# Turning the queries of twenty token tiles by a DRAM round trip with one transposing transfer

## The chip, the cores and the metric

One core of one Trainium2 chip runs the whole kernel. The metric is device time in microseconds (us) of one execution; the profile's span runs from the first to the last instruction of the program on that core. TensorE (PE in the profile) does the matmuls, VectorE (DVE) and ScalarE (ACT) the work on elements, GpSimd (POOL) one small power per layer norm, and SyncE (SP) issues nearly all transfers.

## The reference

Two layers, each an FNet mixing step and then a PEER mixture of experts, on a sequence of 2048 tokens of width 512, in fp32:

```python
x = x + _A_ref(_layernorm(x), ...)      # y = Cr @ (x^ Wre^T) - Ci @ (x^ Wim^T), all dense
x = x + _B_ref(_layernorm(x), ...)
x = x + _A_ref(_layernorm(x), ...)
x = x + _B_ref(_layernorm(x), ...)

# _B_ref, per token (512 values), 32 heads, 16 + 16 keys, 256 experts:
q = einsum("nd,dhc->nhc", xf, w_q)                   # two halves of 128 for each head
s1, s2 = q1 @ k1.T, q2 @ k2.T                        # 16 scores for each half
i1, i2 = the two largest of s1, of s2                # 4 candidate sums and expert numbers
top_s, top_e = the two largest of the 4 candidates
g = softmax(top_s)
out = sum over heads and the two: g * gelu(xf . u[top_e]) * v[top_e]
```

## The kernel before

**Tiling.** The sequence is cut in 16 token tiles of 128 tokens. A layer is a list of nine units (`units`, in the order `ORDER[layer]`): seven of 256 tokens, which hold two token tiles each, and two of one token tile. `seq_unit` does the DFT along the sequence for one unit: for each of the 16 row blocks it loads a piece of the DFT matrix (`raw`), splits it on ACT and DVE in a high and a low part (`ch`, L458; `cl`, L462), and adds up three fp32r matmuls for each of four column blocks (L518). `token_tile` does all the rest for one token tile.

**One token tile.** In order: 24 matmuls for the DFT along the width (L668); the residual and a layer norm; the normed rows turned (for most tiles by a 32x32 block transpose on DVE, a store to `xdr` and four loads back, L722 to L745); scores against the folded keys (24 matmuls, L784 and L788); the experts' inner products with all 256 rows of u (L818) and their gelu; then on DVE a long chain that finds the two largest scores of each half (L880 to L926) and leaves in `q`, a [128 tokens, 3, 2, 2, 32] fp16 tile, for each of 128 picks (2 x 2 x 32) of each token the code of its first key, the code of its second key and its weight. These three 128x128 matrices are **the queries** of the change: picks lie along the free axis and have to come to the partitions. `f_pq` (L1015) turns them by three fp16 transposes on TensorE into a PSUM tile from the pool `bank`, and `f_qt` (L1020) copies that on ACT, rearranged, to the SBUF tile `qt`. From `qt` DVE makes four one-hot masks and two products (`f_m` and `f_w`, L1041 and L1047), TensorE multiplies them in 32 small matmuls (`f_blocks`, L1057), ACT takes the result out (L1089), and a second round trip through DRAM (`gdr`: two stores, L1116, and two loads, L1124) brings the expert weights into rows. These weight the gelu values (L1131); the product is turned (L1162) and multiplied with v (L1181, L1185), or, for most tiles of layer 1, put off to the end of the kernel.

**What sets the order.** Nothing is scheduled by the compiler. Each step is an `Op` of a `Plan` (`op(engine, us, fn, after, take, last, prio, lag, behind, shy)`): its engine, a written-in duration `us`, what it comes after, which buffers of a pool it takes and gives back, a priority, for transfers a `lag` until the data is there, and a further margin `shy` for those who use it. `Plan.run` plays this list forward in time, on each engine the step that can start first, by priority among equals, and never more than eight transfers in flight; the steps are then issued in the order of their planned starts. So each engine's order, SyncE's queue included, is fixed before the kernel runs; at run time an engine that comes to a step early waits there, and everything behind it in its queue waits too. A matmul step of a middle tile is planned another 0.8 us (`WARY`) after what another engine gives it. The matmuls of `seq_unit` have the lowest priority and fill TensorE between the steps of the token tiles.

The pools that the change touches or adds to: `bank` (4 PSUM banks), `q` (2 buffers), `qt` (1); beside them `raw` (4 loaded DFT pieces) and `c` (3 converted ones, of 12 matmuls each).

Of the kernel before, what the change touches and what calls it, by code (L numbers as in the profile page):

```python
# [11 lines left out]
F16 = mybir.dt.float16  # L12
# [4 lines left out]
P = 128  # L17
# [7 lines left out]
SP = 1  # L25
# [13 lines left out]

def MOVED(layer, at):  # L40
    return at >= 2 if layer == 0 else at < NCH + NSC * (TPC - 1) - 2


def DEFERRED(layer, at):
# [33 lines left out]
class Plan:  # L78
# [10 lines left out]
    def op(self, engine, us, fn, after=(), take=(), last=(), prio=(0, 0), lag=0.0, behind=(), shy=0.0):  # L89
        o = Op(len(self.ops), engine, us, fn, [a for a in after if a is not None], list(take), list(last), prio, lag,  # L90
               list(behind), shy)
        for h in o.last:
            h.users += 1
        self.ops.append(o)
        return o
# [60 lines left out]
MM512, MM256, TR32, TR16, MMG = 0.230, 0.121, 0.110, 0.057, 0.026  # L156
# [6 lines left out]
def act(n):  # L163
    return 0.09 + n / 1.2e3
# [7 lines left out]
def spectral_peer_kernel(ctx: ExitStack, tc, x_in, cseq, ctile, dhid, wq, k1t, k2t, ut, vm, out):  # L172
    nc = tc.nc
# [4 lines left out]
    dram = ctx.enter_context(tc.tile_pool(name="dram", bufs=1, space=bass.MemoryType.DRAM))  # L178
# [1 line left out]


    BUFS = {"acc": 4, "bank": 4, "raw": 4, "c": 3, "p": 1, "row": 4, "wr": 5, "wp": 2,
            "tok": 3, "sc": 1, "eq": 1, "act": 3, "q": 2, "top": 1, "qt": 1, "lr": 4, "gt": 1, "pp": 1, "gdr": 2, "xdr": 2, "bn": 1, "pick": 1}
    plan = Plan(BUFS)


# [41 lines left out]
    def work(shape, dtype, name, pool=None):  # L228
        return work_pool().tile(shape, dtype, name=name, bufs=BUFS[pool or name])
# [7 lines left out]
    op = plan.op  # L237
# [368 lines left out]
    last = {}  # L606
# [3 lines left out]
    def token_tile(layer, n, i, t0, at):  # L610

        prio = (0, layer, at if at < len(units) - 1 else -1 - layer, i)
# [5 lines left out]
        t = {}  # L618
# [6 lines left out]
        a = None  # L625
# [31 lines left out]
        for cs in wide:  # L657
            hb, nc_ = Hold("bank"), cs.stop - cs.start
            for z, (k, ms) in enumerate(steps):
                def f(z=z, k=k, ms=ms, cs=cs):  # L660
# [4 lines left out]
                    for c in range(2):  # L665
# [6 lines left out]
                a = op("PE", 2 * len(ms) * (MM512 if nc_ == D else MM256), f, [pready[layer, n][k][2 in ms], a] + dft_done + seed,  # L672
                       take=[hb] if z == 0 and not fine else [], behind=[a_row],
                       last=[phold[layer, n]] if z == len(steps) - 1 else [], prio=prio)
# [11 lines left out]
        if fine:  # L686
            a = ln_rest(lambda: t["bn"].rearrange("p a b -> p (a b)"), hbn, i, bn_done, prio)
        else:
            a = ln_stats(lambda: t["row"], i, [b] + ([xready[1, i]] if (1, i) in xready else []), prio)
# [60 lines left out]
        for z, k in enumerate([] if moved else ks):  # L750
# [16 lines left out]
            hb = Hold("bank")  # L767
            a = op("PE", (k.stop - k.start) * TR32, f_tr, [xn[z]], take=[hb], last=[hx], prio=prio)
# [7 lines left out]
        for hf in range(2):  # L776
            hb = Hold("bank")
# [21 lines left out]
            if fine:  # L799
                for z, k in enumerate(ks):  # L800
                    a_pe = op("PE", 2 * (k.stop - k.start) * MM512, lambda f=f_pch, hf=hf, k=k: f(hf, k), [a_th[z], a_pe],
                              take=[] if z else [hb], prio=prio)
# [8 lines left out]
        hb, hact, hg = Hold("bank"), Hold("act"), Hold("act")  # L811
# [13 lines left out]
        a = op("PE", 12 * MM256, f_xu, [a_pe], take=[hb], last=[hth, htl], prio=prio)  # L825
        a = op("ACT", act(N), f_act, [a], take=[hact], last=[hb], prio=late)
# [6 lines left out]
        a = op("ACT", act(N), f_g0, [a], take=[hg], prio=late)  # L833
        a = op("ACT", act(N), lambda: nc.scalar.activation(t["g0"], t["g0"], AF.Copy, bias=1.0), [a], prio=late)
        a = op("DVE", dve(N), lambda: nc.vector.tensor_mul(t["g0"], t["g0"], t["act"]), [a], prio=late)
        a = op("ACT", act(N), lambda: nc.scalar.activation(t["g0"], t["g0"], AF.Tanh, scale=C0), [a], prio=late)
        a = op("ACT", act(N), lambda: nc.scalar.activation(t["g0"], t["g0"], AF.Copy, bias=1.0), [a], prio=late)
# [3 lines left out]
        heq, hq, htop = Hold("eq"), Hold("q"), Hold("top")  # L841
# [91 lines left out]
        if fine:  # L933
            left, a_val, a_key, first = [], [], [], []
            for f in range(2):
                part = slice(f, f + 1), slice(f * H, (f + 1) * H), 32
                order_ = prio + (f,)
                a = largest(0, *part[1:], lambda f=f: t["pc", f], scored[f:f + 1], order_, **hold, behind=first)
# [5 lines left out]
                a = eq(0, *part[1:], view, a, order_)  # L944
                a = code(0, *part, a, order_)
                left += without(*part, view, a, order_, last=banks[f:f + 1], take=[] if f else [hsc])
                hold = {}
                a = tree32(1, *part[1:], left[f:], order_)
                a_val += a
                a = eq(1, *part[1:], lambda c=part[1]: flat("sc")[:, :, c], a, order_, last=[hsc])  # L950
                a_key += code(1, *part, a, order_)
        else:
            a = tree32(0, cols, w, sc_parts, prio, **hold)
            a = eq(0, cols, w, lambda: flat("sc"), a, prio)
            a = code(0, fs, cols, w, a, prio)
            a = without(fs, cols, w, lambda: flat("sc"), a, prio)
            a_val = tree32(1, cols, w, a, prio)
            a = eq(1, cols, w, lambda: flat("sc"), a_val, prio, last=[hsc])
# [48 lines left out]
        c5 = op("DVE", 0.13, lambda: nc.vector.tensor_sub(t["q"][:, 2, :, 1], t["gw"], t["q"][:, 2, :, 0]), [c4], last=[htop], prio=prio)  # L1007
        d0 = op("DVE", 0.1, f_df, a_key, prio=prio)
        d1 = op("DVE", 0.1, lambda: nc.vector.tensor_mul(t["df"], t["df"], t["cc"]), [d0, b6], prio=prio)
        d2 = op("DVE", 0.15, f_sel, [d1], last=[htop], prio=prio)  # L1010


        hb, hqt = Hold("bank"), Hold("raw" if fine else "qt")
# [8 lines left out]
            nc.scalar.copy(t["qt"].rearrange("p r (q j) -> p r q j", q=16),  # L1022
                           t["pq"].rearrange("p r (j q) -> p r q j", q=16))

        a = op("PE", 3 * TR16 + 0.06, f_pq, [c5, d2], take=[hb], last=[hq], prio=prio)
        a_qt = op("ACT", act(384), f_qt, [a], take=[hqt], last=[hb], prio=prio)

        def row_of(r, hf):
            m = t["qt"][:, r].rearrange("p (a b) -> p a b", b=4)[:, 16 * hf:16 * hf + 16]
# [6 lines left out]
        for hf in range(2):  # L1036
            for r in range(2):
# [6 lines left out]
                a = op("DVE", dve(1024, 2), f_m, [a_qt], take=[] if fine and r else hls[-1:], prio=soon)  # L1044
# [48 lines left out]
        if fine:  # L1093
            pe = [op("PE", 16 * MMG + 0.15, lambda hf=hf: f_blocks((hf,)), [made[hf]], take=hbs[hf:hf + 1],
                     last=hls[2 * hf:2 * hf + 1], prio=prio) for hf in range(2)]
# [3 lines left out]
        for hf in range(2):  # L1099
            if fine:  # L1100
                own = [op("DVE", 0.7, f_mask, xn[-1:], prio=late)] if hf == 0 else []
                evac.append(op(("ACT", "DVE")[hf], (1.26, 0.75)[hf], f_own(hf), pe[hf:hf + 1] + own, behind=evac, take=[] if hf else hgs[:1],
                               last=hbs[hf:hf + 1], prio=prio))
# [5 lines left out]
        moves, back = [], []  # L1109
        for hf in range(0 if fine else 2):  # L1110
            def f_out(hf=hf):
                if hf == 0:
                    t["gdr"] = dram.tile([2, E, 4, ROW], F32, name="gdr", bufs=BUFS["gdr"])
                d = t["gdr"][0]
                d = bass.AP(d.tensor, d.offset + hf * 8 * STEP, [[ROW, P], [STEP, 8], [1, 4 * E]])
                nc.sync.dma_start(d, t["gs", hf].rearrange("p g t e -> p g (t e)"))  # L1116
            moves.append(op("SP", 0.6, f_out, evac[hf:hf + 1], behind=moves[-1:], take=[] if hf else [hd], last=[hgs[hf]], prio=prio, lag=2.7))
        for j in range(0 if fine else 2):
            def f_in(j=j):
                if j == 0:  # L1120
                    t["gt"] = work([P, E, E], F32, "gt")
                d = t["gdr"][j]
                d = bass.AP(d.tensor, d.offset, [[STEP, 64], [4 * ROW, E], [1, E]])
                nc.sync.dma_start(t["gt"][j * 64:(j + 1) * 64], d)  # L1124
            back.append(op("SP", 0.6, f_in, moves, behind=back, take=[] if j else [hgt], last=[hd], prio=prio, lag=3.2, shy=0.5))
        if fine:
            a = op("PE", PICKS, f_picks, evac, take=[hgp], last=hgs[:1], prio=prio)
            a = op("DVE", dve(N), lambda: nc.vector.tensor_mul(t["act"].rearrange("p (e f) -> p e f", f=E), t["act"].rearrange("p (e f) -> p e f", f=E),
                                                               t["gp"].rearrange("p f e -> p e f")), [a, a_act], last=[hgp], prio=prio)
        else:  # L1130
            a = op("DVE", dve(N), lambda: nc.vector.tensor_mul(t["act"], t["act"], t["gt"].rearrange("p e f -> p (e f)")),  # L1131
                   back + [a_act], last=[] if deferred else [hgt], prio=prio)

        hb, hpp = Hold("bank"), Hold("c" if fine else "pp")
# [40 lines left out]
        hb = Hold("bank")  # L1175
# [169 lines left out]
```

## Time and profile before

| | us |
|---|---|
| median of 3 runs (lowest to highest) | 1233.59 (1233.14 to 1234.08) |
| the profiled execution | 1233.48 |
| its span | 1231.7 |
| TensorE busy in it | 1220.1 |
| VectorE busy | 1000.1 |
| ScalarE busy | 492.2 |
| transposes of the queries on TensorE (96, of which 60 belong to the twenty tiles) | 11.0 |

The durations of matmuls in the profile overlap, because they are pipelined: a matmul of 512 columns is listed with 0.39 us, but the next one starts 0.23 us later. What a matmul costs TensorE is read from the starts of its neighbours. The profiled execution's time and the median of the runs differ by 0.11 us; the span leaves out 1.8 us of the profiled execution's time.

### The profile page before, as it was taken

The numbers are of one execution on the slowest core, as the hardware profiler recorded it, in microseconds if no ns is written. First come the engines' busy times: TensorE is split into PE (matmuls) and PEld (weight loads), VectorE is DVE, ScalarE is ACT, GpSimd is POOL, SyncE is SP. The second block draws the span as 40 slices with busy tenths as digits, with TensorE's granted clock in tenths as the row PEclk, the third lists the DMA queues.
The fourth block names the chain that finished last, engine by engine and source line by source line (L and its number), as shares of the span: only waits on it lengthen the run. The fifth ranks groups of instructions, "written<-read, shape, count | busy, mean of one in ns | idle before, by whom it ended". The sixth has DMA issues, their size and how long they took to land. (4 is left out here: it accounts for less than half of the span.)

```text
span 1231.7 us, 20733 instructions
## 1 busy us (share of the span) xinstructions
PE 1220.1 (99%) x7626; PEld 1014.5 (82%) x7626; DVE 1000.1 (81%) x2272; ACT 492.2 (40%) x1010; POOL 45.0 (4%) x71
## 2 busy tenths in 40 slices
PE   9999999999999999999999999999999999999998
PEld 6877778878788888899988988788888888888886
DVE  8899997999897785968987359959596786859796
ACT  7522234334343333324654233334343333343455
POOL 2000000000000000000000000000000000000000
PEclk9999999999999999999999999999999999999999
DMA  7866551453444244441656243563635254454464
GB/s 241 261 200 218 188 169 35 101 119 83 123 122 113 70 116 116 107 120 49 172 142 174 79 120 82 125 135 92 154 97 140 73 145 111 99 141 104 115 204 144
DMA packets 312726, 160.12 MB, mean 130 GB/s; under 512 B 216752, under 2 KB 283056, under 8 KB 312624
## 3 DMA queue, kind: packets, MB, share of 16 engines
q1 hardware_dynamic: 312480, 158.66, 48.2%
q8 instruction: 60, 0.98, 0.3%
q14 instruction: 42, 0.34, 0.1%
q10 hardware_dynamic: 144, 0.13, 0.0%
HBM read 120.73 MB, written 38.01 MB: 129 GB/s over the span
## 5 line engine op out<-in xcount | busy, mean ns | idle before, releaser
L518 PE MATMUL acc<-ch,xh 128*128 128x512 f32 (+1 forms) x868 | 328.3, 378 | 0.8 <-DVE ptl L547 0.8
L518 PE MATMUL acc<-cl,xh 128*128 128x512 f32 (+1 forms) x868 | 321.9, 371 | 0.0
L518 PE MATMUL acc<-ch,xl 128*128 128x512 f32 (+1 forms) x868 | 321.7, 371 | 0.0
L458 ACT CAST ch<-raw 128x512 fp32r<-128x512 f32 x256 | 158.6, 620 | 272.0 <-PE acc L518 222.7
L462 DVE TENSOR_TENSOR cl<-raw,ch 128x512 fp32r<-128x512 f32 x256 | 176.0, 688 | 61.6 <-ACT ch L458 51.4
L518 PEld LDWEIGHTS acc<-cl,xh 128*128 128x128 f32 x868 | 163.6, 188 | 28.8
L518 PEld LDWEIGHTS acc<-ch,xh 128*128 128x128 f32 x868 | 163.6, 189 | 28.0 <-issue 1.8
L518 PEld LDWEIGHTS acc<-ch,xl 128*128 128x128 f32 x868 | 163.8, 189 | 25.6
L880 DVE TENSOR_TENSOR tmp<-sc 128x512 f32<-128x512 f32 (+1 forms) x64 | 43.5, 680 | 72.9 <-ACT sc L793 72.6
L784 PE MATMUL bank<-wh,tok 128*128 128x512 f32 x256 | 100.3, 392 | 0.3 <-ACT tok L742 0.3
L784 PE MATMUL bank<-wl,tok 128*128 128x512 f32 x256 | 99.7, 389 | 0.0
L668 PE MATMUL bank<-dh,pth 128*128 128x512 f32 x248 | 98.6, 397 | 0.0
L668 PE MATMUL bank<-dl,pth 128*128 128x512 f32 x248 | 96.7, 390 | 0.0
L668 PE MATMUL bank<-dh,ptl 128*128 128x512 f32 x248 | 93.6, 390 | 0.0
L793 ACT COPY sc<-bank 128x512 f32<-128x512 f32 x62 | 36.1, 588 | 138.1 <-PE bank L788 108.0
L1041 DVE TENSOR_TENSOR lr<-iota,qt 128x1024 f16<-128x1024 f16 x124 | 81.0, 686 | 12.0 <-ACT qt L1022 11.9
L260 POOL TENSOR_TENSOR stats<-stats,half 128x1 f32<-128x1 f32 x64 | 43.7, 689 | 1149.1 <-DVE stats L257 1135.1
L867 DVE TENSOR_TENSOR eq<-sc,val 128x1024 f16<-128x1024 f32 (+1 forms) x64 | 77.2, 1207 | 1.5
L518 PE MATMUL acc<-ch,xg 128*128 128x512 f32 (+1 forms) x204 | 77.3, 379 | 0.0
L518 PE MATMUL acc<-cl,xg 128*128 128x512 f32 (+1 forms) x204 | 75.7, 371 | 0.0
L518 PE MATMUL acc<-ch,xm 128*128 128x512 f32 (+1 forms) x204 | 75.7, 371 | 0.0
L788 PE MATMUL bank<-wh,tok 128*128 128x512 f32 x256 | 68.4, 389 | 0.0
(190 smaller groups left out, 2057.8 us busy)
## 6 DMA issues: line engine op xcount, KB each, us to landing
raw<-in_cseq SPq DMA_DIRECT2D x224, 256.0 KB, 2.8
wr<-in_wq SPq DMA_DIRECT2D x32, 512.0 KB, 3.8
gdr<-lr SPq DMA_DIRECT2D x62, 256.0 KB, 3.7
raw<-in_ctile SPq DMA_DIRECT2D x32, 256.0 KB, 2.9
xdr<-lr SPq DMA_DIRECT2D x25, 256.0 KB, 2.8
tok<-xdr SPq DMA_DIRECT2D x100, 64.0 KB, 2.6
wr<-in_x SPq DMA_DIRECT2D x16, 256.0 KB, 3.3
row<-in_x SPq DMA_DIRECT2D x16, 256.0 KB, 4.0
```

Of the source, the lines that this page charges most:

```text
L260: nc.gpsimd.tensor_tensor(st[:, 1:2], st[:, 1:2], half, op=ALU.pow)
L458: nc.scalar.copy(t[1], t[0])
L462: nc.vector.tensor_sub(t[2], t[0], as32(t[1]))
L518: nc.tensor.matmul(target(d), w[s][:, d * P:(d + 1) * P], moving(s % per, part), start=(s == 0 and k == 0 and d % blocks == 0), stop=(s == ...
L668: nc.tensor.matmul(t["y", cs.start], w[:, k, c, t0:t0 + P], r[:, c, k, cs], start=(not fine and z == 0 and c == 0 and m == 0), stop=(z == ...
L784: nc.tensor.matmul(t["pc", hf], t["th"][:, k, :], r[:, k, hf], start=(k == 0 and r is wh), stop=False)
L788: nc.tensor.matmul(t["pc", hf], t["tl"][:, k, :], wh[:, k, hf], start=False, stop=(k == KD - 1))
L793: nc.scalar.copy(t["sc"][:, :, hf, :], t["pc", hf].rearrange("p h e -> p e h"))
L867: nc.vector.tensor_tensor(t["eq"][:, :, cols], scores(), val(rank_, cols), op=ALU.is_equal)
L880: nc.vector.tensor_max(t["tmp"][:, :, cols], flat("sc")[:, :8, cols], flat("sc")[:, 8:, cols])
L1041: nc.vector.tensor_tensor(t["m", hf, r], io2, row_of(r, hf), op=ALU.is_equal)
```

## The change

For the units at places 2 to 6 of either layer's order (`Q_MOVED`), all of two tiles, so for 2 x 5 x 2 = 20 of the 32 token tiles, `f_pq` is not called. Instead SyncE issues a store of `q` to a DRAM tile `qdr` (3 matrices of 128 tokens by 128 picks; runs of 256 bytes, 96 KB), waits for it, and issues one transfer with `transpose=True` that reads the 384 x 128 fp16 elements back as 128 x 384 into a new SBUF tile `qi`. `f_qt` then copies from `qi`, and no longer from PSUM; what follows is as before. The plan is told 0.45 us and a lag of 2.3 us for the store, and 0.5 us, a lag of 3.0 us and a margin of 0.5 us for the load. The other twelve tiles keep the transposes on TensorE.

```diff
+def Q_MOVED(layer, at):
+    return 2 <= at < 7
...
-            "tok": 3, "sc": 1, ... "gdr": 2, "xdr": 2, "bn": 1, "pick": 1}
+            "tok": 3, "sc": 1, ... "gdr": 2, "xdr": 2, "qi": 1, "qdr": 2, "bn": 1, "pick": 1}
...
-        a = op("PE", 3 * TR16 + 0.06, f_pq, [c5, d2], take=[hb], last=[hq], prio=prio)
-        a_qt = op("ACT", act(384), f_qt, [a], take=[hqt], last=[hb], prio=prio)
+        if Q_MOVED(layer, at):
+            hqi, hqd = Hold("qi"), Hold("qdr")
+
+            def f_out():
+                t["qdr"] = dram.tile([3, P, P], F16, name="qdr", bufs=BUFS["qdr"])
+                nc.sync.dma_start(t["qdr"].rearrange("r t c -> t r c"), t["q"].rearrange("p r k a h -> p r (k a h)"))
+
+            def f_in():
+                t["pq"] = work([P, 3, P], F16, "qi")
+                nc.sync.dma_start(t["pq"].rearrange("p r t -> p (r t)"), t["qdr"].rearrange("r t c -> (r t) c"), transpose=True)
+
+            a = op("SP", 0.45, f_out, [c5, d2], take=[hqd], last=[hq], prio=prio, lag=2.3)
+            back = [op("SP", 0.5, f_in, [a], take=[hqi], last=[hqd], prio=prio, lag=3.0, shy=0.5)]
+            a_qt = op("ACT", act(384) + 0.05, f_qt, back, take=[hqt], last=[hqi], prio=prio)
+        else:
+            a = op("PE", 3 * TR16 + 0.06, f_pq, [c5, d2], take=[hb], last=[hq], prio=prio)
+            a_qt = op("ACT", act(384), f_qt, [a], take=[hqt], last=[hb], prio=prio)
```

More of the change, by code (lines that the diff above doesn't have):

```diff
@@ L182, in spectral_peer_kernel @@
     BUFS = {"acc": 4, "bank": 4, "raw": 4, "c": 3, "p": 1, "row": 4, "wr": 5, "wp": 2,
-            "tok": 3, "sc": 1, "eq": 1, "act": 3, "q": 2, "top": 1, "qt": 1, "lr": 4, "gt": 1, "pp": 1, "gdr": 2, "xdr": 2, "bn": 1, "pick": 1}
+            "tok": 3, "sc": 1, "eq": 1, "act": 3, "q": 2, "top": 1, "qt": 1, "lr": 4, "gt": 1, "pp": 1, "gdr": 2, "xdr": 2, "qi": 1, "qdr": 2, "bn": 1, "pick": 1}
     plan = Plan(BUFS)
```

## The prediction

> **What bounds the kernel now.** I read the page's first part, then stretches of the span, then who waits on TensorE.
>
> ```profile
> span 1231.7 us, 20733 instructions
> PE 1220.1 (99%) x7626; PEld 1014.5 (82%) x7626; DVE 1000.1 (81%) x2272; ACT 492.2 (40%) x1010; POOL 45.0 (4%) x71
> core 0: us, PE busy (x) PEld busy (x) DVE busy (x) ACT busy (x) POOL busy (x), PEclk, DMA share, GB/s
> 0.00:290.00 290.00, 285.15 (x2058) 228.48 (x2059) 269.93 (x538) 117.64 (x230) 20.61 (x32) 1.00 0.56 167
> 290.00:610.00 320.00, 318.79 (x1943) 270.22 (x1942) 259.01 (x622) 121.41 (x253) 13.16 (x19) 1.00 0.42 108
> 830.00:1150.00 320.00, 320.00 (x1745) 264.01 (x1744) 248.09 (x578) 118.04 (x248) 4.85 (x9) 1.00 0.46 114
> ```
>
> The twenty tiles' transposes lie in the stretches 290 to 610 us (layer 0) and 830 to 1150 us (layer 1). There TensorE is busy 318.79 of 320 and 320.00 of 320 us, at a full clock, while DVE has 61 and 72 us to spare and ACT some 200 in each. So TensorE's own work is the time: what leaves its queue shortens the span, as long as nothing new makes it wait.
>
> **What the transposes cost TensorE.** The group of L1018 shows 223 ns for one, but that is a pipelined length. The cost is read from the starts around a group of three, in the timeline (start, us, engine, line), at one tile among 512-column matmuls and at one behind 256-column matmuls:
>
> ```profile
> L1018 PE MATMUL bank<-ident,q 128*128 128x128 f16 x96 | 11.0, 223 | 0.4 <-DVE q L985 0.3
> 353.17 0.39 PE L518 MATMUL acc<-ch,xh 128*128 128x512 f32 x1
> 353.40 0.39 PE L518 MATMUL acc<-ch,xl 128*128 128x512 f32 x1
> 353.62 0.39 PE L518 MATMUL acc<-cl,xh 128*128 128x512 f32 x1
> 353.85 0.34 PE L1018 MATMUL bank<-ident,q 128*128 128x128 f16 x3
> 354.00 0.48 PE L518 MATMUL acc<-ch,xh 128*128 128x512 f32 x1
> 354.32 0.39 PE L518 MATMUL acc<-ch,xl 128*128 128x512 f32 x1
> ...
> 428.04 0.28 PE L818 MATMUL bank<-ul,tok 128*128 128x256 f32 x1
> 428.16 0.28 PE L818 MATMUL bank<-uh,tok 128*128 128x256 f32 x1
> 428.28 0.34 PE L1018 MATMUL bank<-ident,q 128*128 128x128 f16 x3
> 428.43 0.47 PE L518 MATMUL acc<-ch,xh 128*128 128x512 f32 x1
> 428.74 0.39 PE L518 MATMUL acc<-ch,xl 128*128 128x512 f32 x1
> ```
>
> At the first, two steps without transposes take 0.45 us (353.17 to 353.62) and the two steps that hold the three transposes take 0.70 (353.62 to 354.32): 0.25 us more. At the second, 428.16 to 428.74 is 0.58 us; without the transposes it would hold one step of 0.12 (428.04 to 428.16) and one of 0.225, so 0.235 us more. I take 0.24 us for a tile, 80 ns a transpose. Twenty tiles: **-4.8 us** on the engine that sets the time. The ends by the two readings are -4.7 and -5.0.
>
> **What it adds.** Two SyncE issues, a wait of SyncE between them, and a chain from `q` to `qt` that is longer by a round trip. The nearest rows are the two round trips that the kernel has: each tile's `gdr`, and `xdr` in 25 tiles (KB each, median us to landing; then one line's issue time in ns and its landing as min/median/max):
>
> ```profile
> gdr<-lr SPq DMA_DIRECT2D x62, 256.0 KB, 3.7
> tok<-xdr SPq DMA_DIRECT2D x100, 64.0 KB, 2.6
> x2d<-row SPq DMA_DIRECT2D x16, 256.0 KB, 2.0
> gt<-gdr SPq DMA_DIRECT2D x62, 64.0 KB, 3.0
> ptd<-pp SPq DMA_DIRECT2D x52, 64.0 KB, 2.2
> wr<-in_dhid SPq DMA_DIRECT2D x4, 512.0 KB, 4.5
> L1116 SPq DMA_DIRECT2D gdr<-lr x62: 366/418/1491, 221.5 to 1207.4; - x62
> DMA to landing us min/median/max: 2.6/3.7/5.1
> L735 SPq DMA_DIRECT2D tok<-xdr x100: 562/628/845, 268.3 to 1101.6; - x100
> ```
>
> *The store* (96 KB, runs of 256 B) lies between `x2d<-row` at 2.0 and `gdr<-lr` at 3.7, which has the same runs and 2.7 times the bytes; `ptd<-pp`, 64 KB in shorter runs, is nearest, at 2.2. I take 2.5 us. *The transposing load* has no row at all. As a plain load of its size it would take 2.6 to 3.0 (`tok<-xdr`, `gt<-gdr`); the slowest median of the table is 4.5, and no row bounds it above. I take 3.3, little over the plain loads of its size, and keep 2.6 and 4.5 as ends for the forecast. Round trip: 5.8 us (4.6 to 8.2).
>
> The plan in the code allows 0.45 + 2.3 for the store, 0.5 + 3.0 + 0.5 for the load and two hops of 0.1: 6.95 us. At 5.8 the data comes 1.15 us early. Between data and TensorE there is more cover, as the small matmuls L1057 of `f_blocks`, the first on TensorE to need `qt`, stand behind DVE's last product L1047 with a margin (the plan's 0.8 us of `WARY` and a hop):
>
> ```profile
> 433.53 0.69 DVE L1047 TENSOR_TENSOR lr<-lr,qt 128x1024 f16<-128x1024 f16 x1
> 435.45 0.69 PE L1057 MATMUL bank<-lr 128*64 128x64 f16 x32
> ...
> 456.54 0.67 DVE L1047 TENSOR_TENSOR lr<-lr,qt 128x1024 f16<-128x1024 f16 x1
> 458.64 0.69 PE L1057 MATMUL bank<-lr 128*64 128x64 f16 x32
> ```
>
> The margins are 435.45 - 434.22 = 1.23 and 458.64 - 457.21 = 1.43 us; I use 1.3. So a round trip of up to 6.95 + 1.3 = 8.25 us costs TensorE nothing, and beyond that each us late is one us of TensorE for each tile. The upper end, 8.2, is just inside.
>
> *Who waits behind the new wait.* SyncE stands about 2.5 us at the load until the store is in; loads of DFT pieces are queued behind it. ACT comes to the copy to `qt` and waits if the data is late, with casts `ch` (L458) behind it; DVE then waits at L1041, with `cl` (L462) behind it. All three lead to the matmuls L518. The cover is the queue of pieces:
>
> ```profile
> L458 ACT CAST ch<-raw 128x512 fp32r<-128x512 f32 x256 | 158.6, 620 | 272.0 <-PE acc L518 222.7 <-issue 21.3 <-PE bank L518 14.2
> ...
> ACT ch L458 <- DMA raw<-in_cseq: 5.7, 4, 2.7
> SPq L1124 <- DMA gdr<-lr: 44.5, 29, 3.8
> ```
>
> ACT waits 222.7 us for TensorE to give a converted piece back, so in general two are ready ahead, 2 x 12 x 0.227 = 5.4 us of matmuls. SyncE stands 29 times, up to 3.8 us, at the same kind of wait for `gdr`, and ACT has waited for a piece's data only 5.7 us in the whole span. I cost these waits at nothing; without the cover it would be 2.5 us a tile, 50 us in all.
>
> *What round trips cost TensorE in practice.* Its waits at the first matmuls behind such trips, and two rows for the small items below:
>
> ```profile
> L1162 PE MATMUL bank<-identf,act 128*128 128x128 f32 x38 | 7.5, 278 | 1.2 <-DVE act L1131 1.2
> L784 PE MATMUL bank<-wh,tok 128*128 128x512 f32 x256 | 100.3, 392 | 0.3 <-ACT tok L742 0.3
> L544 ACT CAST pth<-acc 128x512 fp32r<-128x512 f32 x62 | 36.4, 587 | 36.4 <-PE acc L518 36.3
> q1 hardware_dynamic: 312480, 158.66, 48.2%
> ```
>
> TensorE waited 1.2 us at L1162 behind `gdr`, over 18 tiles (38 transposes, two a tile, less the last tile, which has no such trip), and 0.3 us at L784 behind `xdr`, over its 25 tiles (100 loads, four a tile): 1.5 / 43 = 0.035 us a trip, so **+0.7 us** for twenty.
>
> *Small items together, at nothing.* SyncE issues 40 more transfers at 0.42 and 0.63 us, 21 us of a queue that mostly waits. The copy to `qt` reads SBUF instead of PSUM, about 33 ns dearer by 620 against 587 (0.7 us over twenty tiles, on an engine busy 40%). The 3.9 MB are 2.5% on 158.66 MB, at 48.2% of the transfer engines. `q` is held some 2.5 us longer, with two buffers. A bank of PSUM comes free earlier, but no wait above is for one; it could gain at most the 1.2 us that TensorE idles in the layer 0 stretch. The whole order is planned anew, so steps move that the change doesn't name; I have no row for that but those idle times, and it goes into the chances.
>
> **Sum.** Span 1231.7 - 4.8 + 0.7 = 1227.6; the 1.8 us around it (1233.48 for the profiled execution) give 1229.4; the median of the runs lies 0.11 above that execution: **1229.5 us**. Its own range is 1227.5 (no added wait, and the 1.2 us of idle gone too) to 1231.1, which is 0.2% below before. That 2.5 us is about what a measurement of this kernel can tell from no change.
>
> **Rivals.** *A, the transposing load is slow (slower).* If the load carries its three 128-column blocks one after another, each at the price of a small transfer of its own, it takes 3 x 2.2 = 6.6 us (the `ptd` row). The trip is then 2.5 + 6.6 = 9.1, and TensorE waits 9.1 - 8.25 = 0.85 us at L1057 of every tile, 17 us: 1229.5 + 17 = 1246.5. It decides from a load of about 5.95 us, where 20 x 0.2 us eat the gain; slower by 0.2% from 6.1 (20 x 0.33). For it: no row shows a transposing load. Against it: it would have to land later than any median here, later than even the slowest `gdr` store (5.1).
> The Trainium skill speaks for A. "VectorE: DVE Perf Modes", section "The three transpose paths", gives 1309 ns for a 128x128 bf16 transpose by DMA and 390 ns on TensorE, and its rules advise TensorE where PSUM will do. Three such blocks on top of a plain load of 2.6 us would be an estimated 6.5 us, and the time about 1244.5. The trace does not bear out its TensorE figure for this use: 80 ns each in a running queue. "Advanced Engine Details and Errata", section "X-Bar Transpose (TRN2)", says the contrary for DMA, that such transfers are as fast as regular ones; by that the time is 1229.5. No run here shows either.
>
> *B, the gain is eaten (no change).* The chain grows by 5.8 us, so `f_m` and `f_w` of a unit's second tile, six DVE steps of 0.69 us, move into the next unit's layer norms and block transposes, and these come later. If TensorE waits 0.1 to 0.35 us a tile for that, 2 to 7 us come back: 1231.1 to 1236.1, middle 1233. For it: in 0 to 290 us, where DVE is 93% busy, TensorE idles 4.85 us. Against it: the 61 and 72 us that DVE has spare.
>
> *C, SyncE's queue is held (slower).* If the transposing issue and its wait hold SyncE for more than the 5.4 us of pieces ahead, matmuls L518 starve. At 6.4 us it is 1 us a tile, 20 us: 1249.5. Against it: issues of 0.42 and 0.63 us, and four more pieces in `raw`.
>
> **Chances.** Forecast 0.58: TensorE is full where the change acts, and the round trips here cost almost nothing. B 0.18. A 0.18, for want of any row of such a load. C 0.06. So faster 0.58, no change 0.18, slower 0.24. Of A, half lies over 1246; with C 0.15 is left out above, and 0.04 below 1227.5. Range 1227.5 to 1246.
>
> **What the profile after would show.** L1018 with 36 instead of 96 transposes, the busy time of TensorE in the two stretches still over 99.5%, `qi<-qdr` landing within 4.5 us, ACT's waits for it under some 10 us in all, and no wait of PE at the small matmuls: right. PE waits at L1057's successor released by DVE, together over 4 us: A. Waits of ACT casts for `raw`: C. New PE idle at the score matmuls or the transposes of `act`: B. The most likely way to be wrong is the load's unseen price.

## The result, and the profile after

| | before | changed |
|---|---|---|
| median of 20 runs, us | 1233.93 | 1236.43 |
| lowest to highest | 1233.14 to 1235.36 | 1233.73 to 1237.29 |
| span of the profiled execution | 1231.7 | 1234.8 |

The ratio is 1.0019, with a 95% interval of 1.0013 to 1.0025: the change made the kernel 2.5 us slower, on the very edge of what was called telling from no change. 1229.5 was forecast. Among the runs below, one of the sixteen-tile kernel (3106.65 us) and one of the kernel before (1498.69 us) were slow; the ratios leave them out, and the sixteen-tile median of 1232.39 us would be 1232.24 without that run. All line numbers from L41 on are higher in the changed kernel: by 4 up to the queries, by 19 behind them (the matmuls L518 are L522, the small matmuls L1057 are L1076).

The page's first part and the two stretches in which the transposes lay, of the changed kernel:

```profile
span 1234.8 us, 20688 instructions
PE 1217.6 (99%) x7566; PEld 1012.7 (82%) x7566; DVE 1001.3 (81%) x2272; ACT 498.1 (40%) x1010; POOL 48.7 (4%) x71
...
290.00:610.00 320.00, 318.24 (x1894) 270.83 (x1894) 254.31 (x612) 122.67 (x249) 11.97 (x18) 1.00 0.46 113
830.00:1150.00 320.00, 318.79 (x1712) 263.51 (x1711) 248.72 (x580) 122.73 (x252) 5.39 (x9) 1.00 0.49 121
```

TensorE has 60 instructions fewer and is busy 2.5 us less, but the span is 3.1 us longer. These two stretches lost little: 1.76 us of idle instead of 1.21, and 1.21 instead of none. The rest of the loss lies in a stretch that the prediction didn't quote, the end of layer 0. Before:

```profile
600.00:700.00 100.00, 99.66 (x636) 86.02 (x635) 72.55 (x163) 49.77 (x93) 3.56 (x5) 1.00 0.53 143
```

and after, with who released TensorE there in the view of waits (us in all, times, longest):

```profile
600.00:700.00 100.00, 96.30 (x605) 81.49 (x604) 74.10 (x170) 48.59 (x92) 6.95 (x5) 1.00 0.57 145
...
PE acc L522 <- DVE xl L291: 2.1, 2, 1.7
PE bank L1076 <- DVE lr L1066: 0.8, 1, 0.8
PE bank L788 <- ACT tok L746: 0.4, 1, 0.4
PE bank L1022 <- DVE q L1011: 0.3, 1, 0.3
```

TensorE idles 3.70 of these 100 us, before 0.34. The longest waits are for `xl`, the low part of a normed tile with which layer 1 begins: layer 0's last tiles come in late.

Such idle time understates the loss, for a matmul is listed for 0.39 us and the next could start after 0.23, so each wait hides 0.16 us. I therefore also went from start to start: the time from each matmul to the next, less the median step of its kind in the kernel before. By this measure the changed kernel loses 4.8 us more than before between 600 and 700 us, 1.0 more from 300 to 600, 1.5 more from 750 to 1150, and 0.6 in the rest; with the 4.8 us of the transposes gone (the slower matmul behind each group counted with them), the span grows by 3.1, which is what the page shows. The experiments below use both measures; "lost" is the one from start to start, in one profiled execution each.

Most of the transfers went well. Issues (KB, median us to landing), the issue time of the transposing one in ns with its landing, and the copies to `qt`:

```profile
qdr<-q SPq DMA_DIRECT2D x20, 96.0 KB, 1.8
qi<-qdr SPq DMA_TRANSPOSE x20, 2.4
...
L1038 SPq DMA_TRANSPOSE qi<-qdr x20: 1133/1150/1280, 304.3 to 1144.1; - x20
...
L1026 ACT COPY qt<-qi 128x384 f16<-128x384 f16 x20 | 19.0, 950 | 1.8 <-DMA qi<-qdr 1.8
L1026 ACT COPY qt<-bank 128x384 f16<-128x384 f16 x11 | 5.3, 479 | 5.5 <-PE bank L1022 5.5
L1076 PE MATMUL bank<-lr 128*64 128x64 f16 x992 | 22.3, 197 | 2.8 <-DVE lr L1066 2.1 <-ACT lr L1108 0.7
```

The store takes 1.8 us and the transposing load 2.4, by the medians. But the load issues for 1.15 us, the copy from `qi` takes 0.95 us where the copy from PSUM takes 0.48, and TensorE now waits 2.1 us at the small matmuls for DVE's products. One trip, in the timeline of DVE, ACT and SyncE:

```profile
577.17 0.22 DVE L1011 TENSOR_TENSOR q<-gw,q 128x64 f16<-128x64 f32 x1
577.42 0.39 SPq L1034 DMA_DIRECT2D qdr<-q  x1
579.25 1.15 SPq L1038 DMA_TRANSPOSE qi<-qdr  x1
...
582.92 0.62 ACT L462 CAST ch<-raw 128x512 fp32r<-128x512 f32 x1 [2.25 <-PE acc L522]
583.45 0.95 ACT L1026 COPY qt<-qi 128x384 f16<-128x384 f16 x1
```

The load is issued 1.8 us after the store and its data is there at about 581.6 (579.25 + 2.3), but the order lets ACT do the copy only behind a cast that itself waits 2.25 us for TensorE. Of the 7.0 us from `q` to `qt`, 1.9 are the place in ACT's queue and 0.95 the copy.

One store was slow: that of the second tile to take the trip, issued at 326.79 us, landed after 5.3 us, and the load's data was there at 334.42. That is 8.9 us after `q` was ready (325.55). There ACT waits for the load, DVE for ACT's copy and TensorE for DVE:

```profile
325.32 0.23 DVE L989 TENSOR_TENSOR q<-key,df 128x128 f16<-128x128 f16 x1
...
qdr<-q SPq DMA_DIRECT2D x1, 96.0 KB, 5.3
...
334.44 0.93 ACT L1026 COPY qt<-qi 128x384 f16<-128x384 f16 x1 [1.26 <-DMA qi<-qdr]
335.40 1.89 DVE L1060 TENSOR_TENSOR lr<-iota,qt 128x1024 f16<-128x1024 f16 x3 [3.10 <-ACT qt L1026]
339.76 0.44 PE L1076 MATMUL bank<-lr 128*64 128x64 f16 x16 [0.61 <-DVE lr L1066]
```

These 1.26 us are most of the 1.8 us that ACT waits for loads in all, and the 0.61 us are one of the three waits that make the 2.1 us; the others are 0.80 at 655 us and 0.71 at 1094 us. Why this store is slow is not shown; in the kernels below that move the same tile in the same way it takes about as long (5.0 us in the sixteen-tile kernel).

### The profile page after: what moved, and what is told of

It reads as the page before. It is cut to its first block, busy times and chain, and to the rows that moved or that the text cites. A ratio compares the mean times of both kernels' runs of the same rounds, so it can differ in the third digit from the quotient of the medians.

```text
span 1234.8 us, 20688 instructions
## 1 busy us (share of the span) xinstructions
PE 1217.6 (99%) x7566; PEld 1012.7 (82%) x7566; DVE 1001.3 (81%) x2272; ACT 498.1 (40%) x1010; POOL 48.7 (4%) x71
## 5 line engine op out<-in xcount | busy, mean ns | idle before, releaser
L522 PE MATMUL acc<-ch,xh 128*128 128x512 f32 (+1 forms) x868 | 327.7, 378 | 1.3 <-DVE ptl L551 0.8
L522 PE MATMUL acc<-ch,xl 128*128 128x512 f32 (+1 forms) x868 | 321.9, 371 | 2.1 <-DVE xl L291 2.1
L522 PE MATMUL acc<-cl,xh 128*128 128x512 f32 (+1 forms) x868 | 321.7, 371 | 0.0
L522 PEld LDWEIGHTS acc<-ch,xh 128*128 128x128 f32 x868 | 163.6, 189 | 29.0 <-issue 2.9
L522 PEld LDWEIGHTS acc<-cl,xh 128*128 128x128 f32 x868 | 163.5, 188 | 28.6
L522 PEld LDWEIGHTS acc<-ch,xl 128*128 128x128 f32 x868 | 163.8, 189 | 28.2 <-DVE xl L291 2.8
L264 POOL TENSOR_TENSOR stats<-stats,half 128x1 f32<-128x1 f32 x64 | 47.4, 746 | 1148.6 <-DVE stats L261 992.5
L522 PE MATMUL acc<-ch,xg 128*128 128x512 f32 (+1 forms) x204 | 76.7, 376 | 0.0
L522 PE MATMUL acc<-cl,xg 128*128 128x512 f32 (+1 forms) x204 | 75.6, 371 | 0.0
L522 PE MATMUL acc<-ch,xm 128*128 128x512 f32 (+1 forms) x204 | 75.6, 371 | 0.0
```

Source lines behind the costliest of these rows:

```text
L264: nc.gpsimd.tensor_tensor(st[:, 1:2], st[:, 1:2], half, op=ALU.pow)
L522: nc.tensor.matmul(target(d), w[s][:, d * P:(d + 1) * P], moving(s % per, part), start=(s == 0 and k == 0 and d % blocks == 0), stop=(s == ...
```

## The experiments

Medians of each run's kernel stand beside a kernel before of 1233.8 to 1234.2 in the same call. Theory 1: the last pair of layer 0 alone makes the loss. Theory 2: the end of layer 0 takes back whatever TensorE saved ahead. Theory 3: each moved tile costs, by its transfers and its copy. Theory 4, formed after the first four: the round trips of the pairs next to the end of layer 0 lose there, by the order of work that they force. Theory 6: the waits of middle tiles come from a copy that is longer than the plan counts.

### Where the loss sits: which tiles are moved

**Without the last pair of layer 0.**

```diff
-    return 2 <= at < 7
+    return 2 <= at < (6 if layer == 0 else 7)
```

> 18 tiles take the round trip; the last pair of layer 0 (place 6) keeps its transposes on TensorE. Before is 1233.9, the changed kernel 1236.4. Theory 1 (the loss sits at the end of layer 0, because VectorE idles while that pair's queries are on their way, just where it is the bound): the 4.7 us lost there come back less 0.5 for the two tiles: about 1232.2, and no TensorE idle over 1 us between 640 and 690 us. Theory 2 (what TensorE saves ahead of the end of layer 0 is lost there whatever pair is moved, since the chains of the last four tiles don't get shorter): about 1236 again, with 3 to 5 us of TensorE idle at the layer boundary. Theory 3 (each moved tile costs, by the dearer ScalarE copy of 0.95 us, the SyncE issue of 1.15 us and the waits they make): 18/20 of the loss stays, about 1236.2, with the idle spread over the middle.

1236.43 us, ratio 1.0017 (1.0008 to 1.0026): nothing comes back, so theory 1 falls. The end of layer 0 loses 4.7 us between 600 and 700 us, now with one long wait, and then with a stretch at half the granted clock:

```profile
600.00:700.00 100.00, 97.86 (x614) 83.58 (x613) 74.43 (x169) 49.27 (x93) 3.73 (x5) 0.98 0.53 146
...
PE acc L522 <- ACT xg L290: 1.9, 1, 1.9
...
692.40:695.80 3.40, 3.40 (x9) 2.63 (x9) 0.69 (x1) 0.66 (x2) 0.00 (x0) 0.50 0.00 1
```

The wait ends at 691.4 us; from 692.4 to 695.8 the granted clock is 0.50, the matmuls L522 start 0.43 us apart instead of 0.23, and TensorE loses another 1.7 us. So of the 4.7 us, 1.7 are the clock and not the order by itself.

**Layer 1 alone.**

```diff
+    return layer == 1 and 2 <= at < 7
```

> Ten tiles take the round trip, all in layer 1; layer 0 is as before. Theories 1 and 2 (the loss sits at the layer boundary): no loss there, -2.4 us for the transposes, +1.5 for the two stalls seen in layer 1: 1233.0, at best 1231.5. Theory 3 (each moved tile costs): half of the loss, about 1235.2.

1234.31, ratio 1.0003 (0.9994 to 1.0012). The end of layer 0 is clean (99.64 of 100 us busy), as theories 1, 2 and 4 have it, but the 2.4 us of transposes in layer 1 don't show either: TensorE is busy 317.97 of 320 us there, with new waits at the small matmuls and at one L522 (a third wait, of 0.8 us for `ptl`, is there before too):

```profile
PE bank L1076 <- DVE lr L1066: 1.5, 2, 0.9
...
PE acc L522 <- DVE q L1011: 0.5, 1, 0.5
```

So there are two losses, one at the end of layer 0 and one in the middle of layer 1.

**The last pair of layer 0 alone.**

```diff
+    return layer == 0 and at == 6
```

> Two tiles take the round trip, the last pair of layer 0 (place 6). Theory 1 (this pair makes the loss): +4.7 - 0.5, about 1238. Theory 2 (the saving ahead of the boundary is what is lost there): nothing saved ahead, so 1233.4 to 1234. Theory 3 (each moved tile costs): +0.25, about 1234.2.

1235.93, ratio 1.0015 (1.0007 to 1.0024). Two tiles alone lose 2 us, half of what theory 1 expected, and against theory 2, for nothing was saved ahead. The waits are others again:

```profile
600.00:700.00 100.00, 97.31 (x616) 83.11 (x615) 74.04 (x165) 48.68 (x93) 2.74 (x5) 1.00 0.56 147
...
PE bank L1022 <- DVE q L989: 1.5, 1, 1.5
PE bank L1181 <- DVE act L1150: 0.9, 1, 0.9
```

**Sixteen tiles: without places 5 and 6 of layer 0.**

```diff
+    return 2 <= at < (5 if layer == 0 else 7)
```

> Sixteen tiles take the round trip: places 2 to 4 of layer 0 and 2 to 6 of layer 1. Theory 2 (the end of layer 0 takes back whatever TensorE saved ahead of it): the 1.4 us saved in layer 0 are lost there, the rest as with layer 1 alone: 1234.3. Theory 4 (the round trips of the two pairs next to the end of layer 0, places 5 and 6, lose the time, because their late steps fall in among the chains of the last four tiles): no added idle between 600 and 700 us, 1234.3 - 1.4 = 1232.9, or up to 0.8 more for the two waits seen at 339 and 352 us.

1232.39, ratio 0.9986 (0.9977 to 0.9995): faster than before. TensorE doesn't idle at all at the end of layer 0:

```profile
600.00:700.00 100.00, 100.00 (x638) 86.23 (x638) 74.17 (x165) 49.19 (x92) 2.89 (x5) 1.00 0.53 143
```

This kernel differs from the one without the last pair only in place 5 of layer 0, which is worth 4.0 us; 1.7 of these are the half clock behind the long wait there, as far as the one profiled execution tells (over whole executions the granted clock is 0.997 to 1.000 without the last pair, mostly 0.998, and 0.999 to 1.000 with sixteen tiles). Theory 2 falls, and theory 4 stands, with a time a little under its 1232.9.

**Place 5 of layer 0 alone.**

```diff
+    return layer == 0 and at == 5
```

> Two tiles take the round trip, place 5 of layer 0 alone. With places 2 to 5 the end of layer 0 lost 4 us against places 2 to 4. Theory 4 (the pair itself loses, as place 6 alone does): 1235 to 1238, with added TensorE idle between 600 and 700 us. Theory 2 in a milder form (not the pair, but what all pairs ahead have saved together, 1.9 us, is too much for the end of layer 0): 1233.5 to 1234, no added idle there.

1235.03, ratio 1.0012 (1.0003 to 1.0021). The pair loses by itself, as place 6 does, at the low end of what was expected, again at the end of layer 0:

```profile
600.00:700.00 100.00, 97.51 (x619) 83.65 (x617) 73.57 (x165) 49.64 (x93) 4.25 (x5) 1.00 0.55 146
...
PE bank L672 <- ACT pth L548: 1.5, 1, 1.5
PE bank L1022 <- DVE q L989: 1.0, 1, 1.0
```

**Places 2 to 4 of layer 0 alone.**

```diff
+    return layer == 0 and 2 <= at < 5
```

> Six tiles take the round trip, places 2 to 4 of layer 0, costs as in the change. By the differences so far (sixteen tiles 1232.4, the ten of layer 1 alone 1234.3) it should stand at 1232.1; by the transposes alone, 6 x 0.24, at 1232.6, less the waits at 339 and 352 us and more the one at 321 us that went: 1233. If layers don't add up: 1234 or more.

1232.74, ratio 0.9994 (0.9985 to 1.0003): 1.0 us less than the kernel before of the same call, at 99.96 of 100 us busy at the end of layer 0. By the medians that lies between what the transposes save (1.4) and that less the waits (0.7, since 1.1 and 0.5 us come and 0.9 goes); its interval holds no change.

### What makes it: the order, the transfers, or the saving

**The delays in the plan, the transposes on TensorE.**

```diff
-            a = op("SP", 0.45, f_out, ...)
-            back = [op("SP", 0.5, f_in, ...)]
+            a = op("SP", 0.45, lambda: None, ...)        # same lags, margins and holds
+            back = [op("SP", 0.5, lambda: None, ...)]
+            a = op("PE", 3 * TR16 + 0.06, f_pq, back, take=[hb], last=[hqi], prio=prio)
```

> The plan counts the same delays for the twenty tiles, but nothing is transferred: the three transposes are done on TensorE after the planned delay, with the copy from PSUM as before. It is the longer chain in the order of work without the transfers. Theories 1 and 2 (order and chain length lose the time): the loss stays and the 4.8 us of transposes return: about 1241. Theory 3 (the transfers, their issue and the dearer copy cost): about as before, 1234 to 1235.

1238.63, ratio 1.0037 (1.0024 to 1.0049). Without a byte moved, a changed order alone loses 4.7 us against before, and TensorE is busy 96.51 of the 100 us at the end of layer 0. Theories 1 and 2 expected 1241, theory 3 1234 to 1235; the loss is nearer to the order's, not at its number. But it is a third order, since the transposes are steps of the plan again and come after the delay: TensorE's steps are not in the changed kernel's order. Here too a long wait, 2.4 us until 654.3 us, is followed by 3.4 us at a granted clock of 0.50, worth another 1.7 us in this execution. So this run doesn't tell what the changed kernel's own order costs.

**Layer 0's ten transposes left out, no delay.**

```diff
+            a_qt = op("ACT", act(384), f_left, [c5, d2], take=[hqt], last=[hq], prio=prio)   # qt <- q, in order
```

> Left out: the transposes of the ten tiles of layer 0 (places 2 to 6); the queries are copied as they are, so the masks hold wrong numbers. Nothing goes through DRAM and the chain is no longer than before; layer 1 is as before. TensorE saves 2.4 us ahead of the end of layer 0. Theory 2: TensorE idles 2.4 us more between 600 and 700 us and the time is 1233.5 to 1234. Theory 4: the saving passes, 1231.5.

1230.86, ratio 0.9972 (0.9962 to 0.9982). TensorE's saving passes the end of layer 0 in full: 3.2 us (2.2 to 4.7 by the interval) against 2.4 expected, with 99.95 of 100 us busy there. So what TensorE saves ahead is not what is lost.

**All twenty left out, the delays kept.**

```diff
+            a = op("SP", 0.45, lambda: None, ...)
+            back = [op("SP", 0.5, lambda: None, ...)]
+            a_qt = op("ACT", act(384) + 0.05, f_left, back, ...)
```

> Left out: the transposes of all twenty tiles, copied as they are, with wrong numbers; the plan still counts the delays of the round trip, so the order of work is that of the changed kernel, but nothing goes through DRAM and the copy is short. Theories 2 and 4 (the order and the longer chain lose the time): the boundary loss stays, 1235 to 1236.4. If the transfers themselves, their late landing or the dear copy lose it: 1233.9 - 4.8 = 1229, with what the plan itself leaves idle at the boundary (2 us) 1231.

1234.70, ratio 1.0003 (0.9994 to 1.0011). This has the changed kernel's delays in the plan, but no transfer and a copy of 0.51 us. Its order is the changed kernel's: in the traces the steps of TensorE, VectorE and ScalarE, the transposes and the copies to `qt` set aside, follow one another line for line as there. The end of layer 0 loses as much as there (6.1 us between 600 and 700 against 5.8), with the same waits at the same places:

```profile
600.00:700.00 100.00, 96.03 (x600) 81.02 (x600) 72.39 (x163) 47.62 (x90) 6.96 (x5) 1.00 0.54 141
...
PE acc L522 <- DVE xl L291: 2.1, 2, 1.6
PE bank L1072 <- DVE lr L1062: 0.8, 1, 0.8
PE bank L1022 <- DVE q L1011: 0.7, 1, 0.7
```

So that loss is the order's, shown; the transfers have no part in it. The transfers with the dear copy make the other 1.7 us (1236.43 - 1234.70), 1.5 of them between 300 and 600 us; that much is left of theory 3. In layer 1 the two new waits of TensorE are the order's too, for they are here as in the changed kernel (0.7 and 0.5 us there):

```profile
PE bank L1072 <- DVE lr L1062: 0.9, 1, 0.9
...
PE acc L522 <- DVE q L1011: 0.7, 1, 0.7
```

In layer 0's middle this kernel has no wait of TensorE in the list at all between 300 and 600 us, where the changed one has two:

```profile
PE bank L1181 <- DVE eq L907: 1.1, 1, 1.1
PE bank L1076 <- DVE lr L1066: 0.6, 1, 0.6
```

The second is the wait behind the slow store; the first comes 13 us after it, and whether it follows from it is not shown.

### What makes the waits of middle tiles

**The copy turned, in the same order of work.**

```diff
+                nc.scalar.copy(t["qt"].rearrange("p r (q j) -> p r j q", q=16),
+                               t["pq"].rearrange("p r (j q) -> p r j q", q=16))
```

> e5_sixteen, in the same order of work, with one change: the copy from qi reads in order and writes rearranged, where it read rearranged and wrote in order. If the 0.95 us of the copy come from reading SBUF at a step of 32 bytes, it falls to about 0.5 us, as for the copy in order in the kernel with the transposes left out. Theory 6: the waits at 339, 352, 932 and 1089 us shrink by up to 0.45 each: 1232.4 - 1.5 = 1231. If the waits come from the order alone: 1232.4.

The copy didn't fall, it doubled: writing at a step of 16 bytes costs more than reading at one of 32.

```profile
L1027 ACT COPY qt<-qi 128x384 f16<-128x384 f16 x16 | 30.9, 1932 | 2.7 <-DMA qi<-qdr 2.7
...
PE bank L1080 <- DVE lr L1070: 2.2, 2, 1.4
PE bank L1185 <- DVE eq L907: 1.1, 1, 1.1
PE bank L1185 <- DVE act L1154: 0.9, 1, 0.9
```

The waits are those of 300 to 600 us. As a dose it serves as well, since TensorE, VectorE and ScalarE go through their steps in the sixteen-tile kernel's order: 0.98 us more of ACT in sixteen tiles give 1236.90, ratio 1.0023 (1.0014 to 1.0033), 4.5 us more than there. A copy that is late by about a microsecond costs TensorE 0.28 us a tile; it is not hidden. The wait of 1.1 us doesn't grow with it.

**The plan told the true costs, sixteen tiles.**

```diff
-            back = [op("SP", 0.5, f_in, ..., lag=3.0, shy=0.5)]
-            a_qt = op("ACT", act(384) + 0.05, f_qt, ...)
+            back = [op("SP", 1.2, f_in, ..., lag=1.5, shy=1.5)]
+            a_qt = op("ACT", act(384) + 0.54, f_qt, ...)
```

> The same sixteen tiles, but the plan is told what the changed kernel's profile shows and a margin: the load issues for 1.2 us, lands 1.5 later and gets a margin of 1.5 (4.2 in all instead of 4.0), and the copy from qi takes 0.95 us instead of 0.46. Theory 6 (TensorE's waits at the small matmuls of three middle tiles come from the copy that is planned 0.5 us too short): those waits go, 2 to 2.5 us less than with the old costs: about 1230.5 with theory 4, 1232 with theory 2. If the waits come from something else: as e5_sixteen, within 0.5 us.

1233.16, ratio 0.9991 (0.9982 to 1.0000). The middle loses less, as theory 6 says: from 300 to 550 us TensorE loses 0.5 us instead of 2.6, from 900 to 1100 0.4 instead of 1.8. But the new order loses 4.7 us between 550 and 700 us, where the old costs lost 0.6. The sum is no better.

**The same costs, layer 1 alone.** The diff is the last one with `return layer == 1 and 2 <= at < 7`.

> The ten tiles of layer 1 alone, with the costs and the margin of e6_sixteen_costed; layer 0 is planned as before, so its end can't move. Theory 6 (the waits at the small matmuls of middle tiles come from the copy that is planned too short, and only the new order at the end of layer 0 hid this in e6_sixteen_costed): the waits at 932, 1089 and 1128 us go, 2.4 us less than before: 1231.7. If they come from the order itself: 1234.3, as with the old costs.

1233.18, ratio 0.9994 (0.9985 to 1.0003). The waits at the small matmuls are gone from the list, but two smaller ones stand in other places, and the time comes 1.0 us under before, not 2.4:

```profile
PE bank L758 <- ACT tok L275: 0.5, 1, 0.5
PE bank L672 <- DVE ptl L551: 0.3, 1, 0.3
```

That the waits go doesn't show theory 6. The kernel with all twenty left out has two of the three in layer 1 as well (at 935 and 1093 us), with a copy of 0.51 us and nothing transferred, so these two are the order's. Telling the plan other costs gave another order, which lacks them. In layer 0 the wait at the small matmuls goes with the transfers and the dear copy together, and the slow store stands before it. So theory 6 fails for two of the waits and is not shown for the others; and whether the time of this layer is better at all is unclear, since this interval and that with the old costs overlap.

**Old costs in layer 0, true ones in layer 1; sixteen tiles.**

```diff
+            back = [op("SP", 1.2 if layer else 0.5, f_in, ..., lag=1.5 if layer else 3.0, shy=1.5 if layer else 0.5)]
+            a_qt = op("ACT", act(384) + (0.54 if layer else 0.05), f_qt, ...)
```

> Sixteen tiles as in e5_sixteen (places 2 to 4 of layer 0, 2 to 6 of layer 1); layer 0 is planned with the old costs, so that its end stays as it was there, layer 1 with the costs and margin of e6_sixteen_costed. Theory 4 with theory 6: 1232.4 less the 1.5 us of waits in layer 1: 1231.0. If the waits come from the order: 1232.4.

1231.18, ratio 0.9975 (0.9965 to 0.9984): 3.0 us faster than before, 0.2 from the number expected, but not all by the way expected. Layer 1's waits went (0.4 us lost from 900 to 1100 us, 1.8 in the sixteen-tile kernel), while the end of layer 0 did not stay as it was: a wait of 0.7 us at 607 us is new. Its interval overlaps the sixteen-tile kernel's, so that it is faster than that one is not shown.

**And without place 2 of layer 0; fourteen tiles.** The same with `return 3 <= at < 5 if layer == 0 else 2 <= at < 7`.

> As g1_split_costs, but place 2 of layer 0, whose two tiles made TensorE wait 0.5 and 1.2 us at 339 and 352 us, keeps its transposes on TensorE: fourteen tiles. +0.5 for two tiles' transposes, -1.7 for the two waits: 1229.8 if the end of layer 0 stays as in e5_sixteen, 1231 to 1234 if the new order makes waits there.

1230.78, ratio 0.9976 (0.9965 to 0.9986). No idle at the end of layer 0 (100.00 of 100 us busy), as in the sixteen-tile kernel, and none of the two waits of place 2; but one at 322 us that the kernel before has is back (0.9 us), and the time is no better than the last one's beyond the interval.

These two beat both kernels: 3.0 and 3.4 us under before, 5.3 and 5.7 under the change as it was made.

## Why the prediction was wrong

**The 4.8 us of the transposes: as far as the runs show, right.** With ten tiles' transposes left out and no delay the time fell by 3.2 us against their 2.4, which lies inside the interval (2.2 to 4.7). That kernel's chain is shorter and its order is planned anew, too, so the 0.8 us more are not assigned.

**"Costs almost nothing", +0.7 us for twenty trips: the step that failed.** It took the waits at the consumers of `gdr` and `xdr` as the price of a trip, and put the order, which is planned anew, among the small items at nothing, with only a share of the chances. Those two trips were in the order already; what a third one costs is not its own wait alone but what it does to the order of all that follows. The new order lost 4.8 us at the end of layer 0, as much as the transposes save, and the same order without transfers lost as much there. In place of +0.7 the trips cost 7.3 us in all (2.5 slower by the medians, with 4.8 saved): besides the end of layer 0 there are the two new waits of layer 1, which are the order's too, and some 1.5 us of transfers and copy in layer 0's middle.

**The cover of 8.25 us: the one trip that tests it fits.** It took 8.9 us from `q` to the data, and TensorE waited 0.6 us at the small matmuls. With the copy 0.47 us longer than was counted, that the figures meet so closely is in part luck. Store and load took 7.6 us of it, inside the 8.2 kept as an upper end, though with a store of 5.3 us where 2.5 was taken. What the sum left out are the 1.2 us until SyncE issued that store, behind two other transfers.

**The stretches that were looked at.** The argument used 290 to 610 and 830 to 1150 us, where the transposes lie, and took DVE's spare time from their means (61 and 72 us). The place that gave way comes behind them, and there the mean hides it; before, at the end of layer 0:

```profile
580.00:600.00 20.00, 20.00 (x189) 19.57 (x188) 19.93 (x53) 10.20 (x20) 0.55 (x1) 1.00 0.61 146
600.00:620.00 20.00, 19.66 (x136) 16.80 (x135) 17.89 (x36) 12.34 (x23) 0.93 (x1) 1.00 0.64 158
620.00:640.00 20.00, 20.00 (x93) 16.32 (x92) 17.54 (x48) 11.78 (x22) 1.53 (x2) 1.00 0.51 147
640.00:660.00 20.00, 20.00 (x127) 16.51 (x126) 18.81 (x47) 13.16 (x28) 0.00 (x0) 1.00 0.57 142
```

and after:

```profile
580.00:600.00 20.00, 20.00 (x195) 19.83 (x194) 19.71 (x48) 12.01 (x22) 0.72 (x1) 1.00 0.50 148
600.00:620.00 20.00, 19.89 (x126) 16.23 (x125) 13.51 (x33) 11.46 (x21) 1.85 (x2) 1.00 0.57 129
620.00:640.00 20.00, 19.28 (x94) 15.77 (x93) 18.80 (x47) 10.94 (x23) 0.00 (x0) 1.00 0.72 174
640.00:660.00 20.00, 18.04 (x106) 14.08 (x105) 19.46 (x47) 11.30 (x21) 4.00 (x1) 1.00 0.42 113
```

Four token tiles' chains run back to back there, and DVE (the fourth figure) is busy 93% over these 80 us. In the changed order it has 4.4 us less to do in 600 to 620 us and is nearly full until 660, while TensorE (the second) runs dry. That this hole in DVE's work is how the pairs lose is only argued: the kernel without the last pair has no such hole (18.42 there) and loses all the same, later, at a wait for `xg` and the half clock behind it. What is shown is that a trip of place 5 or of place 6 loses time there, each by itself, that those of places 2 to 4 don't, and that it takes the order and no transfer. Why the planner's order for exactly these pairs is bad stays open; the first waits are different ones in each case.

**Rival B (the gain is eaten, 0.18) came nearest, but not as it was told.** It put the price at the next unit's layer norms, at 0.1 to 0.35 us in every tile, with a middle of 1233. What came back on the forecast is 6.9 us, twice its middle, and it came at the layer's end and in a few middle tiles. Its 2 to 7 us on 1229.5 would be 1231.5 to 1236.5; the 1231.1 to 1236.1 that it gives are 0.2% to either side of before. That the time lies by that upper end is luck, since the mechanism is another.

**Rival A (a slow load): wrong in its cause.** The load took 2.4 us, below the 3.3 taken and under both ends kept for it; the longest of the twenty took 4.3. "Advanced Engine Details and Errata" of the Trainium skill, section "X-Bar Transpose (TRN2)", has it that such transfers are as fast as regular ones; the runs agree, 2.4 us for 96 KB beside 2.6 and 3.0 for plain loads of 64 KB. The figure of the Trainium skill in "VectorE: DVE Perf Modes", section "The three transpose paths", 1309 ns for one block, doesn't add up over blocks here: three landed in 2.4 us. A's place was hit, though, with waits of TensorE at the small matmuls, 2.1 us in all: 0.6 behind a store of 5.3 us, which the prediction had at 2.5, and the other 1.5 by the order, for they are there with no transfer too.

**The copy, "about 33 ns dearer": mis-sized.** It is 0.47 us dearer (0.95 against 0.48). The rows compared (620 against 587 ns) were of copies that read in order; this one reads 2-byte elements at a step of 32 bytes. "On an engine busy 40%" is no cover by itself either: the dose of 0.98 us cost 0.28 us a tile. What the 0.47 us cost of the changed kernel's time was not measured apart from the transfers.

**Rival C: wrong.** The transposing issue holds SyncE 1.15 us, nearly twice a plain load's 0.63, but TensorE waits for no piece of the DFT matrix in the list, and ACT's casts wait 3.7 us for pieces, before 5.7.

**The signs.** Of those named for the forecast, the load within 4.5 us and ACT's waits of 1.8 us were met. TensorE was busy 99.45% and 99.62% of the two stretches, where both were to be over 99.5%, and there were waits at the small matmuls, where there were to be none. No sign was named for the end of layer 0.

## What to carry to other kernels

When the order of work comes from a planner, a longer chain is priced by the whole new order, above all where a phase ends and several chains run back to back; look at the busiest engine there in short stretches, not in means over the part that is edited. A saving on the engine that sets the time is worth taking only in the places whose order survives it: here places 2 to 4 of layer 0, and layer 1 in the order that the plan made when told other costs there, which together turned +2.5 us into -3.0. Telling the plan the true costs is no cure by itself: in the sixteen-tile kernel it moved the loss to the end of layer 0. To tell an order's price from a transfer's, keep the order and leave the transfer out, and see in the traces that the order is kept. Once a step leaves PSUM for SBUF, check the step width of whoever reads it next.

## What the runs showed of the hardware

- A transposing transfer of 384 x 128 fp16 from DRAM lands in 2.4 us and issues for 1.15 us on SyncE; the plain store of the same bytes issues for 0.38 and lands in 1.8, once in 5.3.
- ACT copies 384 fp16 elements a partition in 0.48 us from PSUM at a step of 32 bytes, 0.51 from SBUF in order, 0.95 from SBUF at 32 bytes, and 1.93 when it reads SBUF in order and writes at a step of 16 bytes. "Advanced Engine Details and Errata" of the Trainium skill, section "Memory Cachelines", says that SBUF wants at least two hits on each 16-byte line; the two reads from SBUF agree with it. It gives no size and doesn't tell reads from writes; here the write costs more.
- The only two waits of TensorE over 1.7 us in the middle of any profiled execution here, of 1.9 us (without the last pair) and 2.4 us (the delays in the plan), were each followed, 1.0 us later and at once, by 3.4 us at a granted clock of 0.50, in which matmuls of 512 columns start 0.43 us apart. Waits of up to 1.7 us were not, nor was one of 2.0 us at the very start of each execution. What decides it these runs don't show.
